# Seven products of a down projection: one whole-array tile against two tiles of half the columns, and a new listing of the tasks

## The chip, the cores and the metric

The kernel runs on one core of one Trainium2 chip. A core has a matrix engine, TensorE (PE), with an array of 128 rows by 128 columns, that writes to PSUM; a vector engine (VectorE, DVE in the profile); a scalar engine (ScalarE, ACT); a general engine (GpSimd, POOL), and SyncE (SP), whose queue starts the DMA transfers here. The metric is the time of one launch in microseconds on the device; lower is better.

## What is computed

Two blocks follow each other. The first is a recurrence with a 40 x 40 state for each of 4 batches and 8 heads, over 768 time steps. The second is a feed-forward block over the 3072 tokens that come out:

```python
for t in range(S):
    y[:, :, t] = einsum('bhd,bhde->bhe', rt, state)
    Sa = einsum('bhde,bhe->bhd', state, at)
    state_decay = state * wt[:, :, None, :] - einsum('bhd,bhe->bhde', Sa, bt)
    state = state_decay + einsum('bhd,bhe->bhde', vt, kt)
...
x = y.transpose(0, 2, 1, 3).reshape(B * S, H * D)      # 3072 x 320
h = x @ w_in                                           # 3072 x 2048
g = h * (1.0 / (1.0 + exp(-1.702 * h)))
out = g @ w_out                                        # 3072 x 320
```

All of it is in fp32.

## The kernel before

**The recurrence** is cut into chunks of 64 time steps. A unit `i` (24 of them) is one chunk of two batches with their 8 heads. For each unit there are: the decays (`decay`, L574), products of keys, values and the like (`prep`, L649), the inverse of a triangular 64 x 64 matrix for each head, made by doubling in five levels (`inverse`, L698; `level`, L772), and the solution with the carried state (`solve`, L872). Nearly all of their matmuls are of 64 x 64 blocks: the array is used as four tiles of 64 rows by 64 columns, and each set of four matmuls has one in each quarter (`QUARTERS`). A level of an inverse goes through several engines: the matmuls (`ps_level`), a copy of the result (L787), a subtraction (L789), a transpose (L738) and a spreading of the transposed blocks (`spread`, L740; it is done by POOL or DVE at L745 or by ACT at L743), and then the next level.

**The feed-forward block** runs in 12 chunks `c` of 256 tokens (two units each). The up product (`up`, L1042) makes 2048 columns of `h` in tasks of four matmuls with 256 columns, in four tiles of 64 x 64. The GELU is on ACT (L1052) and leaves its result in `g_all`. For the first chunk the down product is a plain one in quarters (`plain`, L1056). For the other eleven (`fast`, L1078) the 256 tokens by 2048 times 2048 by 320 product is done as a 2 x 2 block product with seven block products in place of eight, in a form with sums of blocks made beforehand: `combined` (L1084) makes sums of blocks of `g_all` on DVE or POOL, `weight_sums` (L1026) made those of the weights once, `times` (L1093) does the seven products, and `taken` (L1104) copies or adds their results from PSUM into `sb`, from where they are stored.

**The seven products.** Each of the seven is done in two tasks (`h`), each of four matmuls with 128 rows, 128 columns of stationary operand (a 128 x 128 block of `g_all` or of a sum of its blocks, 128 tokens) and 160 moving columns of weights (or sums of weights): the whole array at once. A chunk has 14 such tasks; eleven chunks have 154, with 616 matmuls. In the profile every fp32 matmul stands as two MATMUL records and two LDWEIGHTS records, two passes, so there are 1232 of each under the name `ps_fast`. The results go to two PSUM banks, in columns chosen by `slot`, and `fresh` is set for the first matmul into a bank.

**The order of the work** is written out by hand as one long string, `ORDER` (L111 to L255), made beforehand by a planner that is not part of the kernel. Its 2805 items are all the tasks of the program; each gives the number of the task, the engine (p PE, a ACT, d DVE, g POOL, s SP), and behind it the number of a pair of PSUM banks or, for SP, of how many transfers may be under way. `listed` (L91) reads it, and L1163 to L1165 issue the tasks in that order; each engine runs its own in the order of the listing, with waits between engines where data, buffers or banks make them necessary. The dictionary that `pe_whole` (L336) returns has the prices that the planner uses for a task of the seven products; in this program only the name of the engine is used of it.

All matmuls go through one helper, `mm` (L325), so that they stand under L326 in the profile and are told apart by the name of their PSUM tile: `ps_up`, `ps_fast`, `ps_level`, `ps_B`, `ps_y` and so on. Which part of the array a matmul uses follows from its operands: the number of rows, the number of stationary columns, and the partitions of its output.

The 389 first items of the listing are the opening: constants, first loads, the weights with their re-making, the first units.

Of the kernel before, what the change touches and what calls it, by code (L numbers as in the profile page):

```python
# [130 lines left out]
262p1 570s 513d 588p3 554p2 555a2 589d3 590d3 339s 254p0 556d2 571a 591a3 626d 88d 514a 512g 255p0 263p1 515p2 580g 581g 256d0  # L131
593d 90d 552p3 264p1 257d0 516a2 517d2 592g 583p0 492d 265p1 594g 518d 266p1 553a3 627p2 811s3 267d1 629a2 628a2 410p3 268d1
411p3 412p3 595p1 413p3 584d0 269s2 720p0 597d1 414p3 519a 598d 721a 520p2 415p3 596d1 808s2 416p3 521d2 417p3 522d2 523d
418p3 599g 87d 728s 630p1 432p2 524d 722a0 729s 600p0 419p3 433p2 94d 601d0 434p2 723d 631a1 525p1 527d1 435p2 602d0 569s
436p2 437p2 438p2 528d 603d 420a3 735g 526a1 725s 421p0 443p3 258s 732s 724s4 439p2 529a 530p1 440p2 531a1 92d 809s 422p0
441p2 733d 89d 604a 532d1 533d 534d 444p3 423p0 442a2 424p0 445p3 535p1 541a1 540a1 605p2 572d 538a1 539a1 446p3 425p0 607d2
426p0 608d 606a2 734d 536d1 537d 427p0 428p0 429p0 609a 430p0 610p1 91d 542p2 447p3 543d2 612d1 431a0 448p3 742p0 613d 544p2
449p3 450p3 451p3 452p3 614d 454g 545d2 745a0 557p2 744d0 743d0 611a1 747d 615p1 748d 746g 616d1 558d2 453a3 455d 634p0 620a1
619a1 618d1 635a0 636d0 460p3 617a 457g 461p3 621a1 749p2 559p1 622p0 751d2 750d2 752d 753a 623a0 459g 561d1 560d1 632p2 463p3
456d 780d 736g 624p0 754p1 625d0 633a2 462a3 740p2 562d 637p0 464p3 756d1 469p3 468p3 731s 638d0 757d 470a3 458g 807s 755d1  # L140
639p1 758g 741d2 466d 737d 465d3 799p0 563s 641d1 810s 642d 800a 759p2 643s 761d2 801a0 475p3 472p3 471p3 760a2 640d1 726a
812d 813d 781p0 821p2 473d3 815g 762d 819p1 474p3 802d 477p3 816g 467g 822d2 823d2 824a2 782d0 93d 476d3 783a0 826d 738p0 763a
764p2 766d2 478p3 827a 825g 480p3 965s 765d2 481p3 820d1 564s 644s 739d0 727d 828p1 482a3 479d3 962s 784p0 785d0 814g 953p3
667p2 767d 668p2 805a 484s 954a 830d1 859d 669p2 788p0 670p2 829a1 955a3 789d0 768a 671p2 672p2 967d 963s 860p3 790d0 861a3
769p1 831d 775d1 862a3 1041s 770d1 832a 673p2 674p2 645p3 646p3 647p3 675p2 648p3 833p0 649p3 773d1 772d1 774a1 786p1 834d0
676p2 771a 835d0 650p3 787d1 651p3 677a2 836d 776p1 652p3 817p2 656p0 777a1 958s 657p0 961s 658p0 659p0 653p3 818d2 806d 837g
778p1 838p2 779d1 654p3 840d2 804s 841d 660p0 842g 839d2 655a3 863p1 661p0 968g 662p0 966d 791p3 663p0 843p2 792d3 803s 956g
864d1 845d2 664p0 665p0 959a 793p3 678p1 666a0 679p1 844a2 975p0 846d 680p1 847d 794d3 795d3 976d0 969d 964s 681p1 682p1 848p2
970d 683p1 684p1 685p1 686p1 851a2 687p1 865p3 1013d 977d0 853d2 849d2 483s 854d2 852a2 978d0 688a1 980d 867p0 692g 973p2 850d
866d3 974d2 868a0 855p1 856d1 979g 1040s 695p3 857p2 869d0 858d2 1032p1 689g 1014p0 981a 694g 1016a0 1015d0 696p3 1044s 971p2  # L150
870p0 706p3 796d 691g 1042s 699p3 797s 1033a 871d0 982p0 972d2 1034a1 1035g 983a0 1046d 872p2 984d0 798s 1045g 1195s 873d2
1054p1 1037s 693g 1017p0 985d 707p3 1057d1 697d3 1092d 703p3 874d2 708a3 875d 986a 1055d1 690d 1056d1 1058d 1059d 1048d 704p3
705a3 1198s 698p3 876s 709p3 710p3 877s 987p2 711d3 989d2 1018a0 1060a 701d 1019p0 1047g 957s 988a2 960d 1021p1 1020a0 1049g
1061p2 1186p0 716p3 1187a 1022a1 1036s 702d 713p3 1063d2 1064d 1188a0 990d 991d 1023d1 1062d2 715p3 712p3 992p2 714d3 1190s
1274s 889p0 1065g 1189d 994d2 700d3 995d 1066p1 890p0 717a3 1093p3 1068d1 1069d 1070d 1200d 1191s 891p0 892p0 1192a 1038a
893p0 993a2 894p0 1067a1 1193d 1071p2 895p0 1072a2 996g 896p0 878p1 879p1 1095a3 897p0 898p0 899a0 719s 1194s 1277s 1094d3
1073d2 880p1 1043s 997p3 999d3 881p1 1050p2 998d3 882p1 883p1 1000d 1096p0 900p3 884p1 1001a 901p3 885p1 1074d 886p1 1051d2
1002p2 1097a0 902p3 887p1 1201g 1075d 1076p0 1003d2 1004d 903p3 1078d0 888a1 1077a0 904p3 905p3 1196s 718s 1006a2 1009p1 1199g
906p3 1052p0 1039d 1079d 1005a2 1008a2 1053d0 1010a1 907p3 908p3 1275s 1080g 1007a2 1208p1 909p3 922d 1210d1 1011p0 910a3
1012d0 924d 911p2 1209d1 912p2 1213d 913p2 914p2 1024p3 1211a1 915p2 1081p0 1087a0 1025d3 1086a0 1082d0 916p2 917p2 918p2  # L160
1212g 1026p1 919p2 1085a0 920p2 1084a0 1083a 1027d1 1028d1 1088p0 1098p3 921a2 1099a3 1203d 1100p1 1202g 1089d0 1246d 1214a
1090p0 1101a1 1273s 1091d0 1029g 925d 1102d1 1265p2 928p3 1030s 929p3 1215p0 1103p1 930d3 1266a 1217d0 1104d1 1216a0 936p3
939p3 923d 1267a2 1204p1 1218d 1279d 1105p0 1278d 1205d1 1287p2 927g 1219a 1220p1 1222d1 1288d2 937p3 926g 1106d0 1223d 1431s
931p3 1107d0 938a3 940p3 1281g 1221a1 1280g 1247p0 1289d2 1290d2 1031s 1224a 1276s 1285p2 1271a 1248d0 1268g 1108g 1225p1
942p3 1197s 1286d2 1227d1 1226a1 1282g 1292d 1249d0 943p3 1206p1 1250p2 1291g 1293g 1228d 941d3 1294p0 1207d1 1229g 1109s
1251a2 1272d 932p3 944d3 1230p1 1296d0 1419p2 948p3 1231a1 934g 949p3 1297d 1232d1 1420a 945p3 1233d 935g 946p3 1110s 1234d
1421a2 1252p2 1429s 947d3 1269s 1295a0 1111p1 1253d2 1112p1 1122p0 1235p2 933d3 1236d2 1237g 950a3 1113p1 1254p3 1114p1 1123p0
1428s 1124p0 1115p1 1116p1 1255a3 1241d2 1433d 1239a2 1256d3 1240d2 1298a 1325d 1238a2 1422g 1117p1 1125p0 1299p3 1242p2
1126p0 1243d2 1300d3 1127p0 952s 1128p0 1244p2 1301d3 1245d2 1129p0 1130p0 1427s 1283p3 1423s 1257p2 1131p0 1118p1 1119p1
1120p1 1284d3 1258d2 1259p2 1144p3 1302d 1132a0 1145p3 1121a1 1261d2 1326p0 1260d2 1146p3 1147p3 1262d 1303a 1270s 1304p1  # L170
1328a0 1434g 1306d1 1507s 1430s 1436g 1479d 1327a0 1148p3 1149p3 1435g 1498p2 1305d1 1424s 1150p3 1151p3 1432g 1307d 1499a
1500a2 1308d 1439p0 1133p1 1510s 1664s 1512d 1152p3 1134p1 1153p3 1503s 1440d0 1309p2 1155g 1329p0 1135p1 1311d2 1136p1 1154a3
1137p1 1330a0 1441p0 1442d0 1312d 1138p1 1443d0 1139p1 1333p3 1310a2 1331p2 1446d 1444d0 1334a3 1140p1 1141p1 1313g 1335d3
1142p1 1332a2 1314p2 1315d2 951s 1480p0 1161p3 1143a1 1165p3 1263s 1508s 1320a2 1506s 1481d0 1445g 1318a2 1319a2 1316g 1321p1
1317a2 1504a 1322a1 1437p2 1172p3 1447a 1158g 1162p3 1438d2 1482d0 1323p1 1157g 1511g 1160g 1483p2 1324d1 1520p0 1484d2 1522d0
1156g 1336p1 1523d0 1337d1 1448p2 1450d2 1173p3 1451d 1449a2 1452a 1164p3 1338p2 1521d0 1453p1 1525d 1501g 1340d2 1487p0
1488d0 1526a 1339d2 1455d1 1456d 1489d0 1163a3 1524g 1502s 1740s 1170p3 1169p3 1527p2 1529d2 1454a1 1457a 1518p0 1509s 1171a3
1530d 1174d3 1485p1 1159d 1425a 1519d0 1175p3 1176p3 1528d2 1486a1 1531a 1532p0 1341g 1513g 1168d 1458p1 1558d 1515g 1177d3
1516p2 1534d0 1460d1 1535d 1514d 1426d 1167g 1461d 1264s 1182p3 1178p3 1181p3 1459d1 1342s 1462d 1343s 1533a0 1179p3 1517d2
1660s 1652p1 1662s 1463p0 1344p2 1166d3 1653a 1465d0 1536g 1345p2 1183d3 1346p2 1347p2 1348p2 1464a0 1180d3 1537p0 1539d0  # L180
1349p2 1661s 1667g 1654a1 1559p3 1350p2 1538d0 1665g 1466d 1560a3 1540d 1184s 1541d 1561a3 1467d 1351p2 1352p2 1355p1 1353p2
# [77 lines left out]
def rwkv7_gelu_quick(ctx: ExitStack, tc: tile.TileContext, time_d, v_d, w_d, wc_d, ak_d, b_d, rv_d, w_in, w_out, out):  # L259
# [20 lines left out]
    HALF = [slice(0, 64), slice(64, 128)]  # L280
# [44 lines left out]
    def mm(o, lhsT, rhs, start):  # L325
        nc.tensor.matmul(o, lhsT, rhs, start=start, stop=True, skip_group_check=True)  # L326
# [9 lines left out]
    def pe_whole(n, cols):  # L336

        return {"PE": n * 2 * (2 * cols / 2.4 + 3), "instr": 4 * n, "mode": 1}
# [908 lines left out]
```

## Time and profile before

| | us |
|---|---|
| three timed runs | 683.36, 683.46, 686.85 (median 683.46) |
| the profiled execution | 678.06 |
| its span, first to last instruction | 676.3 |
| busy in the span: PE | 646.6 |
| DVE | 463.6 |
| ACT | 324.9 |
| POOL | 256.8 |
| busy under `ps_up`, 3840 records | 243.2 |

The profile is of one execution. A group of instructions is named by its line, engine, operation, and the tiles that it writes and reads; PEld is the loading of stationary operands, which runs beside the matmuls. The ends of matmuls are modelled, so that records overlap: the distance of their starts is the sounder measure. "issue" stands where an engine waited for nothing that the profile shows. The chain of waits follows the work that ended last backwards, and its shares say which engine held the end.

### The profile page before, as it was taken

The numbers are of one execution on the slowest core, as the hardware profiler recorded it, in microseconds if no ns is written. First come the engines' busy times: TensorE is split into PE (matmuls) and PEld (weight loads), VectorE is DVE, ScalarE is ACT, GpSimd is POOL, SyncE is SP. The second block draws the span as 40 slices with busy tenths as digits, with TensorE's granted clock in tenths as the row PEclk, the third lists the DMA queues.
The fourth block names the chain that finished last, engine by engine and source line by source line (L and its number), as shares of the span: only waits on it lengthen the run. The fifth ranks groups of instructions, "written<-read, shape, count | busy, mean of one in ns | idle before, by whom it ended". The sixth has DMA issues, their size and how long they took to land.

```text
span 676.3 us, 39075 instructions
## 1 busy us (share of the span) xinstructions
PE 646.6 (96%) x17904; PEld 586.3 (87%) x17904; DVE 463.6 (69%) x913; ACT 324.9 (48%) x711; POOL 256.8 (38%) x250
## 2 busy tenths in 40 slices
PE   5778999999999899999999999999999999998997
PEld 5667777999889899889999998988989988998977
DVE  5778887898788677665855587778666766766111
ACT  4677754645653473375365365454175363343020
POOL 6442435153143236236345235334524424342101
PEclk9989999999999999999999999999999999999999
DMA  6886753413334313332304232521341320310100
GB/s 217 278 263 180 235 154 99 136 43 95 94 91 136 111 45 100 111 114 84 108 25 139 91 82 63 160 83 54 125 117 52 110 63 19 104 24 13 57 16 20
DMA packets 35301, 69.54 MB, mean 103 GB/s; under 512 B 5440, under 2 KB 14656, under 8 KB 35136
## 3 DMA queue, kind: packets, MB, share of 16 engines
q1 hardware_dynamic: 35056, 66.95, 32.8%
q8 instruction: 141, 2.31, 1.4%
q14 instruction: 24, 0.20, 0.1%
q10 hardware_dynamic: 80, 0.08, 0.0%
HBM read 59.15 MB, written 7.86 MB: 99 GB/s over the span
## 4 chain that ended last, share of the span: by engine, by line
PE 86%; DVE 6%; DMA 4%; issue 2%; ACT 1%; SPq 1%; ACTq 0%; DVEq 0%
PE ps_up L326 30%; PE ps_fast L326 24%; PE ps_level L326 8%; PE ps_y L326 5%; PE ps_B L326 4%; PE ps_down L326 3%; PE ps_X L326 2%; PE ps_N L326 2%; PE ps_A L326 2%; PE ps_rz L326 1%; PE ps_RV L326 1%; PE ps_zT L326 1%; DMA w_sb<-in_w_in 1%; PE ps_T L326 1%; PE ps_cum L326 1%
## 5 line engine op out<-in xcount | busy, mean ns | idle before, releaser
L326 PE MATMUL ps_up<-xT_all,w_sb 64*64 64x256 f32 x3840 | 243.2, 377 | 2.6 <-issue 1.6
L326 PEld LDWEIGHTS ps_up<-xT_all,w_sb 64*64 64x64 f32 x3840 | 164.3, 133 | 24.3 <-issue 2.4
L745 POOL TENSOR_TENSOR EX<-ES,quads 128x512 f32<-128x512 f32 x27 | 36.4, 1349 | 122.5 <-DVE ES L738 116.3
L326 PE MATMUL ps_fast<-w_sb,g_all 128*128 128x160 f32 x528 | 82.3, 304 | 0.0
L326 PEld LDWEIGHTS ps_fast<-w_sb,g_all 128*128 128x128 f32 x528 | 73.8, 190 | 2.4 <-ACT g_all L1052 0.4
L1052 ACT ACTIVATE g_all<-ps_up 128x1024 f32<-128x1024 f32 x48 | 49.0, 1024 | 49.0 <-PE ps_up L326 48.6
L326 PEld LDWEIGHTS ps_level<-W,EX 64*64 64x64 f32 x2560 | 54.8, 134 | 4.1 <-issue 1.2
L326 PE MATMUL ps_level<-W,EX 64*64 64x64 f32 (+1 forms) x2560 | 54.9, 218 | 0.2 <-DVE W L787 0.2
L789 DVE TENSOR_TENSOR E<-two,ps_level 128x256 f32<-128x256 f32 x80 | 33.0, 414 | 31.7 <-PE ps_level L326 26.9
L326 PE MATMUL ps_fast<-extra,g_all 128*128 128x160 f32 x352 | 53.6, 302 | 0.1
L787 ACT COPY W<-ps_level 128x512 f32<-128x512 f32 x50 | 29.2, 585 | 49.1 <-DVE E L789 28.3
L326 PEld LDWEIGHTS ps_fast<-extra,g_all 128*128 128x128 f32 x352 | 49.1, 190 | 1.4 <-DVE sb L1106 0.4
L1107 ACT COPY sb<-ps_fast 128x160 f32<-128x160 f32 x26 | 7.6, 293 | 83.1 <-PE ps_fast L326 78.1
L1085 POOL TENSOR_TENSOR xT_all<-g_all 128x512 f32<-128x512 f32 x16 | 21.1, 1319 | 64.6 <-ACT g_all L1052 64.5
L743 ACT ACTIVATE EX<-ES,quads 128x256 f32<-128x256 f32 x82 | 37.0, 503 | 13.2 <-DVE ES L738 11.2
L326 PE MATMUL ps_level<-PT,EX 64*64 64x64 f32 (+2 forms) x1280 | 33.1, 239 | 6.6 <-DVE EX L759 3.7
L833 ACT COPY Tc<-ps_level 32x64 f32<-32x64 f32 x130 | 26.3, 203 | 26.7 <-PE ps_level L326 11.9
L326 PEld LDWEIGHTS ps_level<-PT,EX 64*64 64x64 f32 x1280 | 29.0, 141 | 10.8 <-DVE EX L759 3.8
L326 PE MATMUL ps_y<-RV,kh 64*64 64x104 f32 (+1 forms) x768 | 34.7, 249 | 2.6 <-issue 1.6
L738 DVE STREAM_TRANSPOSE ES<-E 128x256 f32<-128x256 f32 x80 | 34.3, 436 | 2.6
L326 PE MATMUL ps_y<-M,bh 64*64 64x104 f32 (+1 forms) x768 | 34.3, 247 | 0.6 <-DVE M L943 0.6
L660 POOL TENSOR_TENSOR ak<-ak,GT 128x512 f32<-128x512 f32 x20 | 26.6, 1331 | 20.3 <-DMA ak<-in_ak 8.9
(152 smaller groups left out, 1369.3 us busy)
## 6 DMA issues: line engine op xcount, KB each, us to landing
ak<-in_ak SPq DMA_DIRECT2D x48, 160.0 KB
rv<-in_rv SPq DMA_DIRECT2D x48, 160.0 KB
time<-in_time SPq DMA_DIRECT2D x24, 320.0 KB
xT_all<-x_dram SPq DMA_DIRECT2D x48, 160.0 KB
wc<-in_wc SPq DMA_DIRECT2D x20, 264.0 KB
logw<-in_w SPq DMA_DIRECT2D x24, 160.0 KB
RV<-in_v SPq DMA_DIRECT2D x24, 160.0 KB
b<-in_b SPq DMA_DIRECT2D x48, 80.0 KB
```

Of the source, the lines that this page charges most:

```text
L326: nc.tensor.matmul(o, lhsT, rhs, start=start, stop=True, skip_group_check=True)
L660: plan.add(R, {"DVE": 690.0, "POOL": 1270.0, "sbuf": True}, lambda t: of(t.engine).tensor_mul(khT(), khT(), GT_of(i)), reads=T("ak", "GT") ...
L738: plan.add(rank, dve(256), lambda t: nc.vector.transpose(ES(n), source(t)), writes=[key("ES", n, 6)], **reads)
L743: nc.scalar.activation(dst[:, :, h], ES(n), ACT.Copy, scale=quads[:, h, :1])
L745: of(t.engine).tensor_mul(dst, ES(n).unsqueeze(2).to_broadcast([128, 8, 2, 32]), quads.unsqueeze(1).to_broadcast([128, 8, 2, 32]))
L787: plan.add(rank, any2(512), lambda t: copy(t.engine)(tiles_of(W(n + 1)), blocks(psum(t, ""), 64)), writes=[key("W", n + 1, 5)], pair=pair)
L789: plan.add(rank, dve(256), lambda t: nc.vector.tensor_sub(tiles_of(E(n + 1)), every(two32, [128, 2, 4, 32]), blocks(psum(t, ""), 64)[:, :, ...
L833: copy(t.engine)(dst, src[:, u, :, f])
L1052: plan.add(-45, {"ACT": 1030.0, "table": "gelu"}, lambda t: nc.scalar.activation(g_of(c * NQ + q).rearrange("p m r n -> p r m n"), psum(t, ...
L1085: plan.add(R + 20 + 2 * h, dict(one), lambda t: of(t.engine).tensor_tensor(out=out(h), in0=x(h), in1=y(h), op=op), reads=gs(h) + reads, wr ...
L1107: else copy(t.engine)(o(), psum(t, "")[bank][:, slot * HD:(slot + 1) * HD]),
```

## The change

In `times` each matmul of 128 stationary columns becomes two, one behind the other, of 64 stationary columns each: tokens 0 to 63 of the block with the output on partitions 0 to 63, and tokens 64 to 127 with the output on partitions 64 to 127. The moving operand is the same for both, with all 128 rows. `fresh` holds for both. The number in `pe_whole` that tells the planner how many instructions a task has is doubled. The listing is a new one from its 390th item on: the same 2805 tasks in all, from there in another order, some of them on another engine and with other PSUM banks.

```diff
@@ -125,133 +125,133 @@
...
-242p1 399p2 502g 249p0 573s4 400d2 80s4 250p0 401d2 74d 503p3 243p1 504d3 547p2 244p1 75d 548a2 389p3 245p1 549a2 338s4 246p1
-247a1 390d3 402p3 82a 251p0 76d 565p2 403d3 574s3 505p1 77g 566a 506d1 404p3 259p1 83d 406d3 407d 405d3 567a2 252p0 587a 508p2
-260p1 550p3 261p1 582d 578d 551a3 85d 575s4 585p3 84d 576s4 491a 408s 409s2 579d 509d2 510d2 730s2 253p0 511a2 568g 586d3 86g
...
+242p1 399p2 502g 249p0 573s4 400d2 80s4 250p0 401d2 74d 503p3 243p1 504d3 547p2 244p1 75d 548a2 389p3 245p1 549a2 338s4 390d3
+246p1 247a1 82a 402p3 251p0 76d 505p1 77g 565p2 403d3 506d1 404p3 566a 587a 83d 405d3 406d3 84d 407d 259p1 252p0 567a2 508p2
+582g 550p3 509d2 575s4 85d 551a3 260p1 339s 261p1 576s4 578d 574s3 585p3 262p1 579d 510d2 491a 511a2 253p0 588p2 86g 586d3
...
+2751a3 2770p2 2774g 2761p1 2771p2 2772p2 2762a1 2776g 2773a2 2777g 2780p3 2783p3 2781p3 2791p3 2792p3 2784p3 2782d3 2778d
+2803s 2804s
...
@@ def pe_whole @@
-        return {"PE": n * 2 * (2 * cols / 2.4 + 3), "instr": 4 * n, "mode": 1}
+        return {"PE": n * 2 * (2 * cols / 2.4 + 3), "instr": 8 * n, "mode": 1}
@@ def times @@
                             fresh = (t.pair, bank) not in begun_banks
                             begun_banks.add((t.pair, bank))
-                            mm(ps[:, slot * HD:(slot + 1) * HD], a[:, q, f], w[:, q, f], fresh)
+                            for b in BITS:
+                                mm(ps[HALF[b], slot * HD:(slot + 1) * HD], a[:, q, f, b * 64:b * 64 + 64], w[:, q, f], fresh)
```

More of the change, by code (lines that the diff above doesn't have):

```diff
@@ L131 @@
[L131 to L154, printed above, removed]
@@ L178 @@
[L178 to L181, printed above, removed]
-1356p1 1542p0 1468p3 1469d3 1354a2 1473a3 1666d 1357p1 1358p1 1359p1 1360p1 1361p1 1474d3 1470a 1472a3 1362p1 1544d0 1543a0
@@ new lines @@
+1134p1 1443d0 1135p1 1136p1 1331p3 1137p1 1442d0 1444d0 1445d 1138p1 1334a2 1335d2 1480p2 1506s 1312d 1332d3 1482a2 1512d
+1139p1 1140p1 1313g 1481a2 1141p1 1446d 1157d 1142p1 1483p2 1447a 1314p0 1320d0 1172p3 1143a1 1484d2 1315d0 1161p3 1318a0
+1316d 1437p2 1511g 1319d0 1321p1 1162p3 1322d1 1164p3 1317d0 1438d2 1158d 1323p0 1513g 1520p1 1448p2 1324d0 1522d1 1336p0
+1450d2 1160g 1521d1 1451d 1165p3 1449a2 1452a 1487p2 1337d0 1524g 1338p0 1168d 1159d 1515g 1523d1 1340d0 1525d 1163a3 1453p1
+1488a2 1455d1 1489d2 1169p3 1341g 1173p3 1661s 1166d3 1526a 1508s 1170p3 1454a1 1501d 1527p1 1425a 1339d0 1167d 1264s 1171d3
@@ new lines @@
+2156a 2258p2 2226p1 2157p0 1876d3 1881p3 2202s 2259a2 1865d3 1963s 2228d1 2229d 2158a0 2227a1 1877p3 2041s 2260a2 1880p3
+2351p1 2159d0 2230a 1882a3 1879d3 2231p0 2160d 2233d0 2215p3 2201s 2042s 2352a 2043p2 2044p2 2216d3 2353a1 2045p2 2046p2
+2047p2 2232d0 2048p2 2161d 2162p0 2054p1 2055p1 2361s 2049p2 2056p1 2057p1 2050p2 2051p2 2058p1 2059p1 2123s 2164d0 2165d
+2234d 2365d 2163d0 2355s 2235g 2166g 2261p3 2236p0 2437s 2060p1 2061p1 2203a 2204d 2052p2 2262d3 2238d0 2237d0 2239d 2053a2
+2240d 2062p1 2359s 2063p1 2167p0 2065p3 2064a1 2168d0 2171d0 2066p3 1884s 2172a0 2241p2 2242a2 2170d0 2067p3 2076p1 2243d2
```

207 lines of the change are left out of this document (112 added, 95 removed).

## The prediction

> **What bounds the kernel now.** I read the page of the profile first, then the waits of TensorE behind the opening, then single stretches of its timeline. TensorE (PE) is the bound:
>
> ```profile
> span 676.3 us, 39075 instructions
> PE 646.6 (96%) x17904; PEld 586.3 (87%) x17904; DVE 463.6 (69%) x913; ACT 324.9 (48%) x711; POOL 256.8 (38%) x250
> PE   5778999999999899999999999999999999998997
> PEclk9989999999999999999999999999999999999999
> ...
> PE 86%; DVE 6%; DMA 4%; issue 2%; ACT 1%; SPq 1%; ACTq 0%; DVEq 0%
> PE ps_up L326 30%; PE ps_fast L326 24%; PE ps_level L326 8%; PE ps_y L326 5%; PE ps_B L326 4%; PE ps_down L326 3%; PE ps_X L326 2%; PE ps_N L326 2%; PE ps_A L326 2%; PE ps_rz L326 1%; PE ps_RV L326 1%; PE ps_zT L326 1%; DMA w_sb<-in_w_in 1%; PE ps_T L326 1%; PE ps_cum L326 1%
> ```
>
> PE is on 86% of the chain that ended last, at the full clock; the changed products, `ps_fast`, hold 24% of the span. The first item of the listing that differs is the 390th of 2805; by counting PE's matmuls it stands at 93.6 us of the span. From there to the end PE waited this long:
>
> ```profile
> PE ps_y L326 <- issue: 1.6, 1, 1.6
> PE ps_up L326 <- issue: 1.6, 1, 1.6
> PE ps_up L326 <- DVE W L787: 0.8, 1, 0.8
> PE ps_zT L326 <- DVE zr L881: 0.6, 1, 0.6
> PE ps_RV L326 <- issue: 0.5, 1, 0.5
> PE ps_B L326 <- issue: 0.5, 1, 0.5
> PE ps_X L326 <- issue: 0.3, 1, 0.3
> PE ps_Q L326 <- DVE Tc L833: 0.2, 1, 0.2
> ...
> PE ps_RV L326 <- ACT Tc L833: 0.2, 1, 0.2
> ```
>
> These are twelve rows (the three left out have 0.2 each), 6.9 us together, no DMA among them: what other engines and queues do in that stretch is almost wholly hidden. So the time moves only with what PE itself spends, or if the new order brings waits that this one hides.
>
> **The change part by part.** Each of the 616 products of 128 rows by 128 columns (154 tasks of 4) becomes two of 128 by 64. A product runs as two passes, so 1232 passes become 1232 pairs, and PE gets 2464 more instructions.
>
> *The pair of tiles in the stream.* Before, a pass of 160 columns comes every 1.09/8 = 0.136 us (the last two rows here start 1.09 apart, with 8 passes between):
>
> ```profile
> 317.65 0.54 PE L326 MATMUL ps_B<-RV,A 64*64 64x104 f32 x16
> 318.01 0.54 PE L326 MATMUL ps_B<-zr,ak 40*64 40x104 f32 x16
> 318.48 2.44 PE L326 MATMUL ps_fast<-extra,w_sb 128*128 128x160 f32 x16
> 320.85 0.69 PE L326 MATMUL ps_level<-PT,EX 64*64 64x64 f32 x32
> ...
> 327.78 1.25 PE L326 MATMUL ps_fast<-w_sb,g_all 128*128 128x160 f32 x8
> 328.87 1.25 PE L326 MATMUL ps_fast<-extra,g_all 128*128 128x160 f32 x8
> ```
>
> No row shows two tiles of 128x64. The nearest is the up product, four tiles of 64x64, two of them on the same rows and side by side in columns, as the new pair will be:
>
> ```profile
> 639.78 17.43 PE ps_up L326 x320
> 657.21 15.43 PE ps_fast L326 x112
> ```
>
> 17.43/320 is 0.0545 us, so four tiles of 256 columns take 0.218; whole passes at 0.136 per 160 columns would take 0.136 x 256/160 = 0.218. Side by side they cost what the whole array costs. The bounds for the pair: 0.136 (both together) and 0.272 (one after the other, 1232 x 0.136 = +167 us). I take 0.136, since it is this row's answer; change of the stream: 0.
>
> *The way in and out of a stretch of products.* In both listings the 154 tasks stand in 51 unbroken stretches, so the number of switches between whole and quartered array is the same. What one costs is in the fence before the last. The sixteen `ps_B` passes take 318.01 - 317.65 = 0.36, so the next would start at 318.37; `ps_fast` starts at 318.48, 0.11 late. Its 16 passes hold PE for 2.37 to 320.85 instead of 16 x 0.136 = 2.17, 0.20 more. Part of that is the first weight load, which nothing hides:
>
> ```profile
> L326 PE MATMUL ps_fast<-w_sb,g_all x528: 299/299/403, 140.3 to 670.1; 128*128 128x160 f32 x176
> L326 PE MATMUL ps_fast<-extra,g_all x352: 299/299/403, 154.9 to 672.3; 128*128 128x160 f32 x176
> ...
> L326 PE MATMUL ps_level<-W,EX x2560: 187/218/267, 118.4 to 614.4; 64*64 64x64 f32 x149, 64*64 64x32 f32 x48
> ```
>
> The columns are shortest, median and longest in ns: the first matmul of a stretch lasts 403 instead of 299, 0.104 us of waiting for 128 columns of weights; the first four behind a stretch, with 64 columns each, last 267 instead of 218, 0.049. The rest of the 0.20, 0.10, is the emptying of the array on the way out, as the 0.11 was on the way in. One stretch thus costs 0.11 + 0.104 + 0.10 + 0.05 = 0.36 us, and 51 of them 18.4 us.
>
> After the change the first load of a stretch has 64 columns per tile, and the four quarters load theirs together in that 0.049 us. I take 0.049 for it: 51 x (0.104 - 0.049) = 2.8 us saved. The emptying I leave: the array still goes from tiles of 64 rows to tiles of 128 rows and back. The bounds here are 0 (a load of 128 rows costs as before) and 18.4 us saved (nothing of a switch remains). On this the Trainium skill's page "TensorEngine Tiling (Array Packing)", section "Key Properties", has a rule: changing the tiling mode, not just the tile, drains TensorE. By it the 0.11 and 0.10 stay and the sum is as I make it; read the other way, with a drain only where the column split changes, they would go. The trace shows the drain for 64x64 against 128x128 (0.11 and 0.10 us); no row shows 64x64 against 128x64.
>
> *The new order.* It moves nearly every task behind the 389th, on all engines, with the 268 transfers on SP's queue (and the pacing numbers behind them) among them. The opening is untouched, and both listings end with 40 up tasks and one unbroken stretch of 14 product tasks, in another order inside. Counts per engine, before to after: DVE 835 to 836, ACT 443 to 437, POOL 201 to 206, PE 1058 in both. The heaviest move is the spreading step of the inverse (L740), 124 tasks: POOL 33 to 40, DVE 38 to 31, ACT 53 in both. Its prices:
>
> ```profile
> L745 POOL TENSOR_TENSOR EX<-ES,quads 128x512 f32<-128x512 f32 x27 | 36.4, 1349 | 122.5 <-DVE ES L738 116.3
> L745 DVE TENSOR_TENSOR EX<-ES,quads 128x512 f32<-128x512 f32 x32 | 25.3, 795 | 0.7
> ```
>
> A task on POOL ends 0.55 us later, but POOL is idle 62% of the span and PE has other tasks listed in between: in both listings any two neighbouring levels of one inverse (80 pairs, from the fifth unit on) have more PE work listed between them than subtraction, transpose and spread take. A spread that came out bare would cost its 0.55, and the level, its copy L787 and the next level would wait behind it. I cost the order at 0. Its bounds: -6.9 us (every wait of the twelve rows gone) and +6.9 (as many again). The transfers moved on SP's queue go with it: none ended a wait of PE behind the opening.
>
> *Instructions.* PE's own come by the queue
>
> ```profile
> q8 instruction: 141, 2.31, 1.4%
> ```
>
> in 141 packets of 16 KB, 256 instructions each; 2464 more are 10 packets more. The five "issue" rows above (1.6 + 1.6 + 0.5 + 0.5 + 0.3 = 4.5 us) are waits for nothing visible, perhaps for such packets. 7% more of them is 0.3 us, lost in the order's bounds. The products go from 2 to 4 instructions per 0.136 us, 29 per us, where the quartered up product already runs 2 per 0.0545 us, 37 per us.
>
> **Sum.** The profiled execution took 678.06 us (span 676.3 and 1.8 around it): 678.06 - 2.8 = 675.3. The three timed runs lie 683.46 - 678.06 = 5.4 us higher in the median, so I forecast 683.46 - 2.8 = 680.7 us.
>
> **The rivals.**
>
> *The switch becomes free.* If 64x64 and 128x64 share enough of the array's setting for the next weights to load under the running matmul, the emptying goes too: 51 x (0.11 + 0.10) = 10.7 us more, 670.0; with every wait for weights gone, 683.46 - 18.4 = 665.1. For it: within quartered work no such loss is seen between `ps_B` rows (0.36 apart and no more). Against it: the row height still changes, and the rule above.
>
> *The order brings waits.* On PE, in the inverses and the solves between the stretches, where the twelve rows lie. With as many waits again as now it gives 680.7 + 6.9 = 687.6. It decides the sign once five spreads come out bare (5 x 0.55 = 2.8). For it: seven more slow spreads on POOL, and packets of instructions met at other places. Against it: the same number of stretches and nearly the same load on each engine.
>
> *The pair does not run side by side.* Slower than before: with tiles one after the other 680.7 + 167 = 848; with only the second tile's weight load bare, 1232 x 0.049 = 60, so 741. It would be the same if the program kept the whole array and gave it half the columns. It decides already at 2.8/1232 = 2.3 ns per pair. Against it stands the up product's 0.218. The skill's page "TensorE: Matmul & The Clock Gate", section "Measured speedup vs the span model", allows some 4 ns for each further tile: 1232 x 4 ns = 4.9 us, an estimate from that page, and the time would be 685.6. The up product, with three further tiles in 0.218 us, shows no such cost, so I give that little.
>
> **How the numbers follow.** Forecast 0.55 (its own range 676.5 to 686, from waits up or down by some 4 to 5 us), free switch 0.15, waits by the order 0.20, pair not together 0.10. A measurement of this kernel can tell about 0.5%, 3.4 us, from no change: faster is below 680.0, slower above 686.9. Of the forecast's 0.55, 0.20 lies below 680.0, 0.33 within, 0.02 above; free switch is faster whole; of the order's 0.20, 0.03 is within; of the pair's 0.10, 0.02 (the few ns). That makes 0.35 faster, 0.38 the same, 0.27 slower. The range 668 to 691 holds the forecast, most of the free switch and of the order's waits; the serial pair and the outermost of the free switch stay outside, about 0.15.
>
> **What would show each step.** Starts of eight product passes: 16 matmuls of 128x64 in 1.09 us is the pair side by side, 2.17 us the serial one. The first matmuls of a stretch near 350 instead of 403 ns show the shorter load. The start of `ps_fast` behind a sixteen of `ps_B` 0.11 late, or on time, decides the drain. The sum of PE's waits behind 93 us against 6.9 gives the order's part. The forecast is wrong if that sum moves by over 4 us, if a stretch of 16 old passes takes less than 2.2 us or more than 2.4, or if the count of stretches in the trace is not 51.

## The result, and the profile after

The changed kernel takes 690.22 us (median of 20 runs, 680.97 to 695.40), the kernel before in the same rounds 683.63 us (20 runs, 679.13 to 688.53). The ratio is 1.0067 with a 95% interval of 1.0039 to 1.0096: slower by 0.4 to 1.0%. The ratios here leave out runs more than 1.5% above the fastest of their kernel; that matters for two kernels below, with 5 of 12 runs left out of each: change_again (1.0075, where the medians alone give 1.0127) and new_order_mended (0.999, where they give 1.0057).

One caution for the reading. The profiled executions are single draws from these spreads: before at 678.06 us is from the low end of its runs, after at 691.52 us from the high end of its own. They differ by 13.5 us, the medians by 6.6 us, and 4.1 us of the pair's difference lies in the opening, whose listing is the same in both: the 390th item stands at 93.6 us before and at 97.7 after. In the eighteen profiles of this document it stands anywhere from 93.6 to 102.7 us, so the sums of waits below, all counted from 93.5 us on, hold a last piece of the opening in most of them.

The page after: span, busy time, the queue of instructions, and the chain of waits by engine.

```profile
span 689.8 us, 41550 instructions
...
PE 650.1 (94%) x19136; PEld 582.2 (84%) x19136; DVE 476.1 (69%) x926; ACT 324.9 (47%) x700; POOL 262.8 (38%) x253
...
q8 instruction: 150, 2.46, 1.5%
...
PE 86%; DVE 5%; DMA 4%; issue 3%; ACT 2%; SPq 1%; DVEq 0%; ACTq 0%
```

PE's busy time went from 646.6 to 650.1 us, the span from 676.3 to 689.8: most of the difference is time in which PE does nothing. On the chain, issue rose from 2% to 3%. The packets of instructions are 9 more.

The products by name and shape (columns: shortest, median and longest in ns, first and last start in us, shape):

```profile
L326 PE MATMUL ps_fast<-w_sb,g_all x1056: 296/300/352, 148.3 to 683.3; 128*64 128x160 f32 x176
L326 PE MATMUL ps_fast<-extra,g_all x704: 298/300/351, 166.6 to 685.4; 128*64 128x160 f32 x176
```

And one stretch of three tasks in PE's timeline (start, time held, operation, count):

```profile
156.78 0.36 PE L326 MATMUL ps_X<-B,T 64*64 64x104 f32 x8
157.07 1.31 PE L326 MATMUL ps_fast<-w_sb,g_all 128*64 128x160 f32 x16
158.21 2.34 PE L326 MATMUL ps_fast<-extra,w_sb 128*64 128x160 f32 x32
160.48 0.69 PE L326 MATMUL ps_RV<-rv 40*64 40x64 f32 x32
```

The three tasks hold PE from 157.07 to 160.48, 3.41 us. Inside a stretch 16 of the narrow matmuls come every 1.09 us, as 8 wide ones did, so that 3.26 us are the products and 0.15 the first weight load and the way out. Before, the two tasks of 2.37 us had 0.20 beside 2.17. In the median of the stretches, counted from the records of starts, 0.19 us became 0.14. The first matmul of a stretch has 351 ns where it had 403. The way in is unchanged: the first product starts 0.148 us behind the last matmul of most tasks before it, and 0.178 behind `ps_B`, in the medians of both profiles.

PE's waits behind 93.5 us (tile and what it waited for: us in all, times, longest):

```profile
PE ps_up L326 <- issue: 3.5, 6, 0.9
PE ps_T L326 <- issue: 1.9, 2, 1.5
PE ps_X L326 <- DVE E L789: 1.5, 1, 1.5
PE ps_A L326 <- issue: 1.1, 2, 0.8
PE ps_level L326 <- issue: 1.0, 2, 0.7
PE ps_fast L326 <- DVE sb L1107: 0.9, 1, 0.9
PE ps_N L326 <- ACT P L728: 0.8, 1, 0.8
PE ps_zT L326 <- ACT g_all L1052: 0.7, 1, 0.7
PE ps_Q L326 <- DVE T L745: 0.3, 1, 0.3
PE ps_Q L326 <- ACT Tc L833: 0.3, 1, 0.3
PE ps_fast L326 <- DVE sb L1108: 0.2, 1, 0.2
```

They sum to 12.2 us against 6.9: issue 7.5 against 4.5, other engines 4.7 against 2.4. Of the rows for other engines of before only the small one of ps_Q for Tc is left, on another engine; there are four new ones of 0.7 to 1.5 us. The starts of PE's records say the same without the modelled ends: from the 390th item to the last matmul it is 578.7 us before and 587.8 after. Gaps of over 0.3 us at the ends of PE's packets of instructions (explained below) make 5.8 and 12.1 us of that, other such gaps 4.8 and 8.3, and 568.1 and 567.4 are left.

### The profile page after: what moved, and what is told of

Same layout as the page of the kernel before. It is cut to its first block, busy times and chain, and to the rows that moved or that the text cites. A ratio compares the mean times of both kernels' runs of the same rounds, so it can differ in the third digit from the quotient of the medians.

```text
span 689.8 us, 41550 instructions
## 1 busy us (share of the span) xinstructions
PE 650.1 (94%) x19136; PEld 582.2 (84%) x19136; DVE 476.1 (69%) x926; ACT 324.9 (47%) x700; POOL 262.8 (38%) x253
## 3 DMA queue, kind: packets, MB, share of 16 engines
q1 hardware_dynamic: 35056, 66.95, 32.1%
## 4 chain that ended last, share of the span: by engine, by line
PE 86%; DVE 5%; DMA 4%; issue 3%; ACT 2%; SPq 1%; DVEq 0%; ACTq 0%
PE ps_up L326 30%; PE ps_fast L326 24%; PE ps_level L326 8%; PE ps_y L326 5%; PE ps_B L326 4%; PE ps_X L326 3%; PE ps_down L326 2%; PE ps_N L326 2%; PE ps_A L326 2%; PE ps_rz L326 2%; PE ps_RV L326 1%; DMA b<-in_b 1%; DMA logw<-in_w 1%; PE ps_zT L326 1%; PE ps_T L326 1%
## 5 line engine op out<-in xcount | busy, mean ns | idle before, releaser
L326 PE MATMUL ps_up<-xT_all,w_sb 64*64 64x256 f32 x3840 | 248.6, 378 | 3.6 <-issue 3.5
L326 PEld LDWEIGHTS ps_up<-xT_all,w_sb 64*64 64x64 f32 x3840 | 161.7, 134 | 31.4 <-issue 7.4
L745 POOL TENSOR_TENSOR EX<-ES,quads 128x512 f32<-128x512 f32 x30 | 40.3, 1346 | 111.8 <-DVE ES L738 95.2
L326 PE MATMUL ps_fast<-w_sb,g_all 128*64 128x160 f32 x1056 | 81.1, 302 | 0.0
L326 PEld LDWEIGHTS ps_fast<-w_sb,g_all 128*64 128x64 f32 x1056 | 70.2, 137 | 2.5 <-issue 0.6
L326 PE MATMUL ps_fast<-extra,g_all 128*64 128x160 f32 x704 | 53.0, 301 | 1.1 <-DVE sb L1107 0.9
L743 ACT ACTIVATE EX<-ES,quads 128x256 f32<-128x256 f32 x88 | 39.8, 502 | 25.9 <-DVE ES L738 25.7
L326 PEld LDWEIGHTS ps_fast<-extra,g_all 128*64 128x64 f32 x704 | 47.4, 137 | 2.1 <-DVE sb L1107 1.1
L655 POOL TENSOR_TENSOR ak<-ak,FT 128x512 f32<-128x512 f32 x17 | 24.9, 1466 | 32.6 <-PE ps_rz L326 11.9
L833 ACT COPY Tc<-ps_level 32x64 f32<-32x64 f32 x110 | 22.2, 202 | 26.3 <-PE ps_level L326 9.6
```

The lines of the kernel that those rows point to most:

```text
L655: plan.add(R, {"DVE": 690.0, "POOL": 1270.0, "sbuf": True}, lambda t: of(t.engine).tensor_mul(ahT(), ahT(), FT_of(i)), reads=T("ak", "FT") ...
L743: nc.scalar.activation(dst[:, :, h], ES(n), ACT.Copy, scale=quads[:, h, :1])
L745: of(t.engine).tensor_mul(dst, ES(n).unsqueeze(2).to_broadcast([128, 8, 2, 32]), quads.unsqueeze(1).to_broadcast([128, 8, 2, 32]))
L833: copy(t.engine)(dst, src[:, u, :, f])
```

## The experiments

### The two parts by themselves

tiles_old_order has the edit in `times` and the listing of before; whole_new_order has the new listing and the product as before.

```diff
tiles_old_order, against before:
+                            for b in BITS:
+                                mm(ps[HALF[b], slot * HD:(slot + 1) * HD], a[:, q, f, b * 64:b * 64 + 64], w[:, q, f], fresh)
whole_new_order, against before:
-247a1 390d3 402p3 82a 251p0 76d 565p2 403d3 574s3 505p1 77g 566a 506d1 404p3 259p1 83d 406d3 407d 405d3 567a2 252p0 587a 508p2
...
+246p1 247a1 82a 402p3 251p0 76d 505p1 77g 565p2 403d3 506d1 404p3 566a 587a 83d 405d3 406d3 84d 407d 259p1 252p0 567a2 508p2
...
```

> The two tiles of 128x64 with the listing of before. Instructions theory: PE's instructions come in packets of 256, and PE stands still where it has used up a packet before the next is there (its stops of over 0.4 us stand at instruction 193 of a 256, 8 times in the profile of before, 19 times in that of the change, and PE goes on 1.2 to 1.6 us after a packet has landed). The old listing was not made for the doubled count: packets whose matmuls last under 3.5 us become 22 instead of 18 behind the opening, which adds some 3 to 5 us of such stops, less the 2.6 us saved at the 51 entries: 0 to 3 us slower than before (ratio 1.000 to 1.004), with over 10 such stops. Order theory: the new listing's own waits between engines are the loss; then this run lacks them and is 2.6 us faster than before (0.996). Tile theory: the pair costs something that its stretches do not show; then this run is as slow as the change (1.007).

Measured: 1.0001 (0.9970 to 1.0031). The 0.996 that the order theory had for it lies outside.

> The whole array with the listing of the change. Instructions theory: the lighter count leaves fewer short packets than before (12 against 18 under 3.5 us): 1 to 3 us faster than before (0.996 to 0.999), with some 5 to 8 stops at packet ends. Order theory: all of the loss and the 2.6 us of the entries on top, 7 to 9 us slower than before (1.010 to 1.013), with waits for other engines in the place of stops at packet ends. Tile theory: as before (1.000).

Measured: 1.0141 (1.0100 to 1.0183), 697.94 us against 688.23 in the same rounds: 9.7 us slower. PE's granted clock (its share of full speed) was the same, 0.9935 and 0.9933 in the mean.

The two kernels unchanged in the same rounds:

> The change once more, for a second profile on the chip of the two others: ratio near 1.007 by every theory. Instructions theory: again over 12 stops of PE at packet ends behind the opening. Order theory: the same waits for other engines as in the first profile (DVE E before ps_X 1.5 us, DVE sb before ps_fast 0.9 us, ACT P before ps_N 0.8 us).

> The kernel before once more, for a second profile: ratio 1.000. Its first profile was of an execution at the lower end (678 us against a median of 683.6). Instructions theory: more stops at packet ends than the 8 of the first, as many as make up the 5 us. Order theory: more waits for other engines instead.

Measured: 1.0075 (1.0035 to 1.0115) and 1.0002 (0.9964 to 1.0040).

So the order is what costs, and the tiles are not: alone they change nothing that can be told, and under the new order the change is even 0.7% below the whole-array product (1.0075 against 1.0141, each within 0.4%). PE's waits of whole_new_order in the same window, the larger rows:

```profile
PE ps_X L326 <- issue: 3.0, 2, 1.7
PE ps_up L326 <- issue: 2.5, 4, 1.3
PE ps_level L326 <- issue: 2.2, 4, 1.1
PE ps_X L326 <- DVE E L789: 1.5, 1, 1.5
PE ps_N L326 <- ACT P L728: 1.1, 1, 1.1
PE ps_fast L326 <- DVE sb L1106: 0.8, 1, 0.8
...
PE ps_zT L326 <- ACT g_all L1052: 0.7, 1, 0.7
```

All rows together have 15.6 us: 10.4 of issue and 5.2 for other engines. In before_again, the kernel before in these rounds, they have 7.7: 5.2 and 2.5. The two profiled executions (698.58 and 685.30 us) lie 13.3 us apart, more than the medians, and the rows show 7.9 of it. By the starts of PE's records, behind the 390th item, it is 594.3 against 580.7 us: 7.4 us of the difference are gaps at ends of packets (15.2 against 7.8), 5.0 other gaps (9.1 against 4.1), and only 1.1 us is left. So the order costs by both kinds of waiting, in this pair some 3 to 2.

### What a row of issue is

PE's waits for issue are not spread evenly. One from the timeline of whole_new_order:

```profile
325.67 0.74 PE L326 MATMUL ps_X<-B,T 64*64 64x104 f32 x23
328.09 0.41 PE L326 MATMUL ps_X<-B,T 64*64 64x104 f32 x8 [1.68 <-issue]
```

PE stops in the middle of a task of 32 matmuls with the same sources and goes on with the last eight 1.68 us later, when no other engine had anything to finish for it. Counted through PE's records, the stop falls behind the 17600th, and in all eighteen profiles every row of issue of PE behind 93.5 us falls a multiple of 256 records apart from there: they are the ends of the 16 KB packets. In 116 stops of ten profiles (four of the old listing, six of the new one) PE went on 1.2 to 1.6 us after the last packet had landed, 1.4 in the median. What a packet meets depends on how long the one before it kept PE busy (stops over 0.45 us behind 94 us, from the records of starts):

| PE's time in the packet before, from its first start to its last | old listing, 4 profiles | new listing, 6 profiles | fewer bytes, 2 profiles |
|---|---|---|---|
| under 3.3 us | 20 stops at 42 ends | 32 at 60 | 7 at 22 |
| 3.3 to 4.4 us | 12 at 253 | 43 at 422 | 2 at 115 |
| 4.4 to 5 us | 2 at 92 | 6 at 108 | 1 at 43 |
| over 5 us | 0 at 112 | 1 at 172 | 0 at 66 |

Behind a packet under 3.3 us about every second end has a stop, in both listings, and both have some ten such packets in each profile. What the new listing has more of is stops behind packets of middling length: 10% of them against 5%.

Among these middling packets, in the ten profiles, the records of the queues tell the two kinds apart. Where a stop followed (55), the next packet's transfer began 2.1 us in the median after PE had entered the packet before, and in the 2 us ahead of it the other queues filled 63% of the 16 DMA engines' time. Where none followed (620), it began after 0.9 us, and they filled 24%. The transfer itself took 1.1 us in both. So a late packet begins late, behind data, and is not slow.

### Fewer bytes

I took bytes off the queues: from the fifth unit on, the loads of rv, time and RV bring only the first eighth of their partitions; the data queue moved 52.61 MB instead of 66.95. The results of those units are not the reference's; the work of the engines is the same.

```diff
-    time_of = lambda i: buf("time", i, [128, 2, DM])
+    time_t, RV_t = several("time", [128, 2, DM]), several("RV", [128, 13, 8, 8])
+    time_of = lambda i: time_t[i % 2]
...
+                    if i >= 4 and name in ("rv", "time", "RV"):
+                        p = slice(p.start, p.start + (p.stop - p.start) // 8)
```

> The kernel before, but from the fifth unit on only an eighth of the partitions of rv, time and RV is loaded (the rest of these tiles keeps the values of earlier units), some 17 of 67 MB less. Transfer theory: PE's instruction packets are late where they queue with other transfers; with fewer bytes PE's stops at packet ends (5 and 9 behind 96 us in two profiles of before, 5.8 and 7.4 us) fall by half, and the time by 2 to 4 us (0.994 to 0.997). Sequence theory: the stops come from how closely PE's own instructions follow, whatever else is under way: the same time as before (1.000) and the same stops.

> The whole array with the new listing and the same loads left out as in the run beside it. The full version was 1.0141 with 16 stops at packet ends (14.8 us). Transfer theory: those fall to 5 to 9, and it comes out at 1.002 to 1.008, at most 5 us above the old listing with the same loads left out. Sequence theory: 1.012 to 1.015, still some 9 us above the old listing with fewer bytes, with 14 or more stops.

Measured: 0.9921 (0.9886 to 0.9956) with the old listing, 1.0027 (0.9992 to 1.0062) with the new one; 5.4 and 7.9 us less than with all bytes. Stops at packet ends came to 5.6 and 5.2 us in the two profiles, where the same listings had 5.8 to 6.5 (before, before_again) and 14.8 us (whole_new_order). So bytes in flight cost time that no engine waits for by name, in both listings. In the new one the stops went with them, one profile against one. In the old one the time fell by more than the 2 to 4 us expected, and the stops did not fall by half; its profile is of an execution at 687.68 us, 4.5 above the median, and does not show where the gain lies. The bytes are not all: the orders still differ by 1.06%, 7.3 us, with the stops equal in the two profiles and 5.0 us of waits for other engines against 2.7.

### The place of the transfers alone

Each of SP's 268 tasks is put at the point of the work at which the other listing has it; all else stays.

> The whole array with the new listing for PE, DVE, ACT and POOL, but each of SP's 268 transfer tasks at the point of PE's work where the old listing has it (as far as its data allows). Transfer theory: the places of the transfers against PE's packet ends make most of the 9.7 us: 1.004 to 1.008 and under 10 stops at packet ends. Sequence theory: 1.012 to 1.015, with 14 or more stops.

> The kernel before with SP's transfer tasks at the points of PE's work where the new listing has them. Transfer theory: 4 to 6 us slower than before (1.006 to 1.009), with over 12 stops at packet ends. Sequence theory: as before (1.000 within 0.003), with 5 to 9 stops.

Measured: 1.0119 (1.0073 to 1.0165) for the new listing with the old points, 1.0030 (1.0002 to 1.0057) for the old one with the new points: 1.5 us less than whole_new_order, which is within the errors, and 2 us more than before, just clear of them. By their ratios both are nearer to the sequence theory. The waits of the first show why so little came of it:

```profile
PE ps_level L327 <- issue: 2.1, 2, 1.7
PE ps_level L327 <- POOL EX L746: 2.1, 1, 2.1
PE ps_X L327 <- DVE E L790: 1.5, 1, 1.5
PE ps_up L327 <- issue: 1.2, 3, 0.7
...
PE ps_T L327 <- issue: 0.7, 2, 0.4
```

Issue came from 10.4 to 4.0 us, but a spread on POOL was late by 2.1 us, behind a product of keys (L661) that now waited for its load, issued at 130.9 us where whole_new_order has it at 116.3. The other listing with the new points has 8.1 us of issue. One profile each, they say that the stops go with the transfers' place; a profile below (new_order_mended) speaks against it.

### Where the ends of the packets fall

In two profiles of one listing many stops fall behind the same instruction. I moved all the ends by half a packet: the 16 products of ps_RV in the sixth unit, at about 108 us, are issued three times, the same result each time.

```diff
-            for e, b in product(BITS, BITS):
+            for e, b in list(product(BITS, BITS)) * (3 if i == 5 else 1):
```

> Whole-array products in the new listing; the 16 products of ps_RV of unit 5, at about 108 us, are issued three times over, which is 128 instructions more (half a packet) and about 0.86 us more of PE. Every later end of a packet of 256 instructions falls half a packet earlier in the work. Theory A (where the packet ends happen to fall in the stream decides the stops, and the new listing had bad luck with them): the stops seen in two of its profiles behind 110 us at the instructions 6337, 9409 and 11201 are gone from their places in the work, and the sum of stops falls from 14.8 to the 6 to 9 us of the old listing: 1.004 to 1.009. Theory B (the new listing brings them wherever the ends fall): the places change, the sum stays at 11 to 17 us, 1.012 to 1.018.

> The kernel before with the same 128 instructions more at the same task. Theory A: another draw of places, the sum of stops anywhere from 5 to 15 us where three profiles of the old listing have 5.8 to 8.5, and the ratio between 1.000 and 1.012. Theory B: the sum stays at 5 to 9 us, and the ratio is 1.001 (0.86 us more of PE), 0.998 to 1.004.

Measured: 1.0100 (1.0057 to 1.0144) and 0.9982 (0.9956 to 1.0009). The stops sum to 14.5 us in the new listing (14.8 before the shift) and to 9.0 in the old one (5.8 and 6.5). The sums are what theory B had; the new listing's ratio lies between A and B, the old one's within B. So the new listing did not merely have bad luck with where its packets end, as far as one profile each can tell.

### Taking the standing waits away

The four longest waits for other engines stand in every profile of the new listing, at the same tasks. Seven items were moved by a few places, for instance the copy of P (task 511) ahead of a logarithm (491) on ACT and PE's score_N (588) behind the next product; a subtraction (1217) ahead of two long DVE tasks (1029, 1246). The diff below runs lines of the listing together.

```diff
-578d 574s3 585p3 262p1 579d 510d2 491a 511a2 253p0 588p2 86g 586d3 513d 554p3 590d2
+578d 574s3 585p3 262p1 579d 510d2 511a2 491a 253p0 86g 586d3 513d 554p3 588p2 590d2
...
-929p3 1203g 1029d 1246d 1216a2 1217d2 1101a0 1102d0 1218d
+929p3 1203g 1216a2 1217d2 1101a0 1102d0 1218d 1029d 1246d
```

> Whole-array products in the new listing, with seven tasks moved by a few places so that the four longest standing waits of PE for another engine lose their cause: ps_X for E (1.5 us in the profile of whole_new_order), ps_N for P (1.1), ps_fast for sb (0.8), ps_zT for g_all (0.7), 4.1 us together. Theory (the new listing loses some 4 us by standing waits and the rest by stops of PE at ends of its packets of 256 instructions): these four rows are gone or under 0.2 us each, the stops stay, and the ratio is 1.0141 - 4.1/688 = 1.008 (1.005 to 1.011). Rival (a wait gives the next packet time to arrive, so what is taken from one comes back as the other): the four rows go, more stops come, 1.012 to 1.016.

> The change as it is (two tiles of 128x64, new listing) with the same seven tasks moved. Theory: 3.9 us less than the change (1.5 + 0.9 + 0.8 + 0.7), 1.0067 - 0.0057 = 1.001 (0.998 to 1.004). Rival (the time comes back as stops at ends of packets): 1.005 to 1.009.

Measured: 1.0061 (1.0028 to 1.0094), inside the theory's range, and 1.0047 (1.0017 to 1.0078), nearer to its rival. The waits for other engines in new_order_repaired:

```profile
PE ps_B L327 <- DVE RV L687: 1.0, 1, 1.0
...
PE ps_level L327 <- DVE EX L746: 0.8, 1, 0.8
...
PE ps_Q L327 <- DVE T L746: 0.5, 2, 0.3
PE ps_level L327 <- ACT EX L744: 0.3, 1, 0.3
PE ps_Q L327 <- ACT Tc L834: 0.3, 1, 0.3
```

The four rows are gone, but two turned into the next wait at the same place, 1.0 in place of 1.1 and 0.8 in place of 0.7: behind the task that PE used to wait for, the next one was late as well. The rows for other engines went from 5.2 to 2.9 us with the whole array, where the ratio fell by more than these 2.3 us, by 0.8% (5.5 us, each ratio within 0.4%). With the tiles they went from 4.7 to 3.0: 1.7 us, near the 1.4 us that 1.0067 and 1.0047 lie apart, though the two intervals overlap.

Why the tasks were late shows when the other engines are read beside PE, here in the profile after, ahead of the waits for P and for sb:

```profile
106.60 3.33 POOL L499 TENSOR_TENSOR w_sb<-w_sb,extra 128x1280 int32<-128x1280 int32 x1 [0.88 <-DVE extra L495]
107.03 3.45 DVE L657 SCALAR_TENSOR_TENSOR b<-b,GT 128x512 f32<-128x512 f32 x1
110.40 0.43 DVE L725 COPY_PREDICATED PT<-within,ps_N 128x256 f32<-128x256 uint32 x1
110.86 0.37 ACT L728 COPY P<-ps_N 128x256 f32<-128x256 f32 x1 [3.59 <-DVE PT L725]
...
222.93 1.72 POOL L1085 TENSOR_TENSOR g_all<-g_all,w_sb 128x512 f32<-128x512 f32 x1
223.68 1.54 DVE L569 TENSOR_TENSOR_SCAN wc<-starts,wc 128x264 f32<-128x264 f32 x1
224.62 1.68 POOL L660 TENSOR_TENSOR ak<-ak,GT 128x512 f32<-128x512 f32 x1
225.14 1.72 DVE L570 TENSOR_TENSOR_SCAN wc<-starts,wc 128x264 f32<-128x264 f32 x1
226.78 0.29 DVE L1107 TENSOR_TENSOR sb<-sb,ps_fast 128x160 f32<-128x160 f32 x1
```

P did not wait for the logarithm. ACT was done with that at 107.3 us and stood idle for 3.59 us, until DVE had made the copy at L725, which stood behind a product of `b` (L657) of 3.45 us, where the median of this line is 0.68. The scans ahead of sb took 1.54 and 1.72 us where their medians are 0.70 and 0.68, and the three tasks ahead of E were stretched in the same way (1.13 and 1.49 at L988 for 0.42, 1.55 at L881 for 0.48). All six began while a task of POOL was under way and ended 0.28 to 0.57 us after it. In the eighteen profiles every DVE instruction that took over 0.25 us longer than the lower quartile of its line and shape, 36 to 53 in each, began and ended in this way. Nine in ten ended that usual time, less 0.10 to 0.14 us, after POOL's task, as if they had begun with its end; no run here takes POOL's tasks away to show it. The delays sum to 27.6 us before and 39.7 after, nearly the whole rise of DVE's busy time from 463.6 to 476.1 us.

### Both causes

Three more moves for these two places (the task 586, RV, ahead of 579, the product of `b` above; 1764 ahead of 1698 and 1738 behind 1699); then the same with SP's tasks at the old points, and POOL's 735 behind 529 for the late spread.

> Whole-array products, the new listing with the seven moves of new_order_repaired and three more, for the two waits that took the place of two of the four there: ps_B for RV (1.0 us) and ps_level for EX (0.8 us). Theory (standing waits for other engines cost what the profile writes beside them): these two go, the rows for other engines come from 2.9 to about 1.1 us, and the ratio is 1.0061 - 1.8/688 = 1.0035 (1.001 to 1.006). Rival (each wait taken away turns into the next one, or into stops at ends of packets): 1.006 to 1.010.

> The same, with the tasks of SP's queue at the points of the old listing as in new_order_old_transfers, and POOL's task 735 moved behind task 529, which was late there and made a wait of 2.1 us. Theory (the other part of the order's cost is stops at ends of packets, and they come from where the transfers stand): the rows of issue come from 10.8 to 4 to 6 us, as in new_order_old_transfers (4.0), and the ratio falls by 5 to 6 us more, to 0.996 (0.993 to 1.000), all of the new order's cost. Rival (the transfers' place matters little, as the 1.5 us between new_order_old_transfers and whole_new_order would say): 1.001 to 1.006.

> The change with the ten moves of new_order_mended and its own transfers. Theory: 1.0047 - 2.2/688 (the rows 1.3 and 0.9 that took the place of others in change_repaired) = 1.0015 (0.998 to 1.005). Rival (another wait or more stops in their place): 1.005 to 1.009.

> The same listing with two tiles of 128x64. Theory: as new_order_mended_old_transfers, less the 2.8 us of shorter loads at the entries, 0.992 (0.989 to 0.997). Rival 1 (the tiles gain nothing, as in the old listing): 0.993 to 1.000. Rival 2 (the transfers' place matters little): 0.999 to 1.004.

| | ratio | interval | median us (before 688.78) |
|---|---|---|---|
| new_order_mended | 0.9990 | 0.9950 to 1.0030 | 692.72 |
| new_order_mended_old_transfers | 1.0006 | 0.9973 to 1.0039 | 689.88 |
| change_mended | 1.0054 | 1.0022 to 1.0086 | 691.81 |
| change_mended_old_transfers | 0.9955 | 0.9926 to 0.9984 | 687.75 |

Removing the second wait by itself showed nothing that can be relied on: the 12 runs of new_order_mended lie between 684.36 and 697.31, and change_mended is where change_repaired was, as its rival had it. With both done the cost is gone: from 1.0141 to 1.0006 with the whole array, from 1.0067 to 0.9955 with the tiles. What the transfers' place does in this is shown with the tiles alone (1.0054 to 0.9955, intervals that do not overlap). With the whole array 0.9990 and 1.0006 do not differ, the latter lies between its theory's range and its rival's, and the profile of new_order_mended, its fastest run, has 2.7 us of issue with the transfers of the new listing. One program can meet few late packets or many: the two profiles of the change have stops of 11.0 and 16.7 us. The waits of change_mended_old_transfers:

```profile
PE ps_up L327 <- issue: 3.2, 3, 1.3
PE ps_level L327 <- issue: 1.6, 4, 0.7
PE ps_T L327 <- DVE zr L979: 1.3, 1, 1.3
PE ps_T L327 <- issue: 0.7, 1, 0.7
PE ps_level L327 <- DVE E L790: 0.7, 1, 0.7
```

Issue is at 5.7 us here, between the 7.5 and 10.4 of the change and the 4.5 of before. Of the versions that do all the work this is the only one whose interval lies below both kernels, 0.2 to 0.7% under the kernel before.

## Why the prediction failed

I forecast 680.7 us and called the same time likelier than a slower one; it came out 690.2, inside the range, near its upper end of 691, and on the slower side.

**The failed step is "I cost the order at 0".** The order alone cost 1.41%, 9.7 us (1.00 to 1.83%), where the bound was +6.9. Two things were wrong in how I came to 0.

First, the cover was tested at one place only: I compared the PE work between neighbouring levels of an inverse with subtraction, transpose and spread. The five bare spreads that were to decide the sign did not come. None of the four long waits of the new listing is for a spread. Three are for tasks that came late behind unrelated work on DVE: a subtraction (E, 1.5), a copy on ACT that waited for DVE (P, 0.8 to 1.1) and a result of the products that DVE had not taken (sb, 0.8 to 0.9). The fourth is a bank held by a GELU (g_all, 0.7) that came behind a table load of 1.28 us. And I took each task at its usual time: the work ahead of the three was stretched to between 2 and 5 times that beside tasks of POOL. An engine with a third of its time free hides work on average and still lets a task be late.

Second, "Instructions" priced the rows of issue by the number of packets: 7% more packets, 0.3 us. The tiles brought 9 packets more, as foreseen (10). But the new listing with the whole array, with not one instruction more, has 10.4 us of issue where four profiles of the old one have 4.5 to 6.4. What counts is not how many packets there are but how many arrive late. Late ones began behind data transfers, which I had left out because none ended a wait of PE: a transfer can hold PE up by delaying its instructions, and no row then names it. That the bytes cost time is shown in both listings; that their new place does is shown with the tiles, and only just in the old listing (1.0030).

**The rival "the order brings waits"** is what happened, at 690.2 where it had 687.6. The sum of the waits, the view named to decide it, moved by 5.3 us, beyond the 4 that I had set. The 6.9 us that its price rested on came from one profile at the low end of the runs.

**The pair of tiles in the stream** was right: 16 matmuls of 128x64 in 1.09 us, and the serial pair fell. The extra few ns per tile, which the Trainium skill's page "TensorE: Matmul & The Clock Gate", section "Measured speedup vs the span model", allows, do not appear in this stream: 1.09 us is the time of the eight wide passes.

**The way in and out** was right in mechanism and size: 351 against 403 ns at the first matmul, 0.14 against 0.19 us for first load and way out in the median of 51 stretches, counted from the records in both profiles. That is 51 x 0.046 = 2.4 us where I had 2.8. The emptying stays, as the Trainium skill's page "TensorEngine Tiling (Array Packing)", section "Key Properties", says of a change of tiling mode; the trace shows it now for 64x64 against 128x64, with the way in unchanged at 0.148 us (0.178 behind `ps_B`) and the 0.10 us left beside a load of 0.05 on the way out. The free switch fell. The gain was not seen in the time with the old listing (1.0001, down to 0.9970). Under the new listings the pairs disagree: the tiles are 0.7% faster in the change and 0.5% faster with both causes removed (1.0006 and 0.9955), a little beyond the joint error, no different in the repaired kernels (1.0061 and 1.0047), and 0.6% slower in the mended ones (0.9990 and 1.0054). The stops in the profile of tiles_old_order are 9.3 us against 5.8 and 6.5, which may be where the gain went; old_order_shift, without the tiles, has 9.0, so that this is not shown.

What stays open: why one execution meets more late packets than another of the same program, how the cost of the order divides between late tasks and late packets beyond the one pair of profiles, and why the orders still differ by 7 us with fewer bytes, of which the two profiles show 2.3 as waits for other engines (4.0 in gaps of over 0.3 us between starts).

## What to carry to other kernels

That each engine's load is unchanged does not make a new order free: go through the tasks that take over a buffer or a bank, and ask what stands ahead of the one before them on its engine, and how long that takes beside the other engines' work at this place. When one such wait is mended, look for the next late task behind it before counting the gain. Where the bound engine waits for "issue" inside a task, look at its packets of instructions and at the transfers beside them, and try the transfers where they were when only the work is to be reordered.

## What was not expected of the hardware

PE stops at ends of its packets of 256 instructions, up to 3.5 us at a time, in every profile here: 4.7 to 16.7 us in all. It goes on 1.2 to 1.7 us after a packet has landed. Work that keeps PE under 3.3 us in a packet is followed by a stop at about half its ends, work of over 5 us at one end in 284 (the two listings with all bytes). Taking 14.3 MB off the loads, with no change to any engine's work, made the kernel 0.8% faster in the old listing and 1.1% in the new one.

DVE instructions that begin while POOL is at work can end late: 36 to 53 in each profile did, by 24 to 41 us in all, one of them taking 3.45 us for 0.68 beside a POOL task of 3.33.
